# Attention values with the exp tiles as stationary operand, V plus a column of ones moving, one normalisation per token, DMA transposes, and three feed-forward PSUM banks

## Chip, cores, metric

One core of a Trainium2 chip. The metric is device microseconds of one execution. "PE" is the tensor engine, "PEld" its weight loads, "DVE" the vector engine, "ACT" the scalar engine, "POOL" GpSimd, "SP" the queue that issues nearly all DMAs. SBUF is the memory in which the tiles lie, PSUM the one that the matmuls write to, dealt out in banks. A matmul has a stationary operand (lhsT in the code), put in place by a weight load, and a moving one (rhs); "columns" are those of the moving one. A quad is four heads of one batch.

## The reference

Batch 4, 8 heads, 768 tokens, head size 64, 16 cluster centroids per head; then a gated feed-forward block on 3072 tokens of width 512.

```python
q_assign = argmax(q_n @ c_n.T);  k_assign = argmax(k_n @ c_n.T)      # per head
scores   = where(q_assign == k_assign, q @ k.T / 8, -1e9)
attn     = exp(scores - max) ;  attn /= attn.sum(-1) + 1e-9
x        = (attn @ v), heads side by side                            # [3072, 512]
out      = (silu(x @ w_gate) * (x @ w_val)) @ w_out                  # d_ff = 1536
```

## The kernel before

Work is cut into 192 units (batch, half of the queries, head, pair of key blocks), 48 to a batch and 24 to a chunk of 384 tokens. A unit is two score matmuls, one exp, and the value matmuls of the unit before it. The feed-forward block of chunk n runs between the units of chunk n+1, so PE always has both kinds of work in its queue. Before a batch's units there is preparation of q and k (transposes, cluster routing, masks).

The value product, with V stationary and the 384 exp columns moving. V stands beside 64 columns of ones, so the denominator comes out already copied to 64 partitions. A 385th column, filled with a tiny constant, sums V for rows in which every key is masked:

```python
def att_values(u, pt):
    ...
    for jj in range(2):
        j = 2 * kp + jj
        nc.tensor.matmul(
            out=acc[:, 0:SH + 1], lhsT=va[:, h % 4, 2 * (j % JH) + j // JH, :],
            rhs=pt[:, jj, 0:SH + 1], start=(j == 0), stop=(j == J - 1))
    if kp == JH - 1:                      # once per head
        ...
        nc.scalar.activation(out=den[n0:n0 + 64], in_=acc[d0:d0 + 64, 0:SH],
                             func=ACT.Identity, bias=eps[d0:d0 + 64])
        nc.vector.tensor_scalar_add(num[n0:n0 + 64], acc[n0:n0 + 64, 0:SH],
                                    acc[n0:n0 + 64, SH:SH + 1])
        if h % 2 == 1: norms.append((num, den, (2 * b + hf) % XR, h // 2))

def normalise(num, den, xc, m):           # once per head pair
    for r in range(JH):
        nc.vector.reciprocal(out=den[:, ts(r, 128)], in_=den[:, ts(r, 128)])
        yield                             # one per unit
    nc.gpsimd.tensor_tensor(out=xall[:, xc, m, :], in0=num, in1=den, op=ALU.mult)
```

Gate and value share a pair of PSUM banks, drawn from the same three pairs as the scores and the preparation:

```python
def ffn_gv(ch, fb):
    gv = psum.tile([128, 2, 512], FP32, name="gv", tag="big", bufs=3)
    # 4 matmuls into gv[:, 0], 4 into gv[:, 1]; then
    # ACT: th = tanh(gv0/2);  DVE: ug = (th+1)*gv0;  DVE: hT = ug*gv1
```

The softmax here doesn't subtract the row's maximum and nothing guards it: scores larger than these inputs give would overflow.

Of the kernel before, what the change touches and what calls it, by code (L numbers as in the profile page):

```python
# [17 lines left out]
def kernel(  # L18
# [32 lines left out]
    XR = 4  # L51
# [17 lines left out]
    def load_quad(qi):  # L69
        b, g = quads[qi]  # L70
        for i in range(4):
            h = 4 * g + i
            ts_ = []
            for src in (q, k):
                t = sb.tile([128, J, 64], FP32, name="qk", tag="qk", bufs=12)
                nc.sync.dma_start(
                    out=t, in_=src[b, h].rearrange("(p j) d -> p j d", p=128))
                ts_.append(t)
            qk_tiles[(b, h)] = ts_

    for s in range(2):
# [7 lines left out]
    NV = 3  # L89
    vaugs = [persist.tile([128, 4, J, 128], BF16, name=f"vaug{i}")  # L90
             for i in range(NV)]

    vst = {}

    def load_v(qi):
        b, g = quads[qi]
        va = vaugs[qi % NV]
        if qi < NV:
            vr = va.rearrange("p (a t) j c -> p a t j c", t=2)
            nc.gpsimd.memset(vr[:, :, 0, :, 64:128], 1.0)  # L100
            nc.gpsimd.memset(vr[:, :, 1, :, 0:64], 1.0)
        for i in range(4):
            t = sb.tile([128, J, 64], FP32, name="vs", tag="vs", bufs=4)
# [5 lines left out]
    def cast_v(qi, i):  # L109
        c0 = 64 * (i % 2)  # L110
        copy(nc.scalar if qi == 0 else nc.gpsimd,
             vaugs[qi % NV][:, i, :, c0:c0 + 64], vst.pop((qi, i)))
# [6 lines left out]
    pts = [persist.tile([128, 2, SH + 2], BF16, name=f"pt{i}")  # L119
           for i in range(NP)]  # L120
    for i in range(NP):
        nc.vector.memset(pts[i][:, :, SH:SH + 2], TINY)
    eps = persist.tile([128, 1], FP32, name="eps")
    nc.vector.memset(eps, S * TINY)
# [32 lines left out]
    def cast_w(i):  # L157
        eng = nc.vector if i % 3 == 0 else nc.gpsimd
# [13 lines left out]
    def prep_head(qi, i):  # L172
# [3 lines left out]
        tp = psum.tile([128, 2, 512], FP32, name="tp", tag="big", bufs=3)  # L176
# [19 lines left out]
    def prep_route(qi):  # L196
        b, g = quads[qi]
        sp = psum.tile([128, 2, 512], FP32, name="sp", tag="big", bufs=3)
# [31 lines left out]
    def prep_mask(qi, i):  # L230
        b, g = quads[qi]
        for par in range(2):
            nc.vector.tensor_copy(  # L233
                out=qkaug[(b, 4 * g + i)][D:KA, par],
                in_=ohTs[qi][32 * i:32 * i + NCL, par])
# [4 lines left out]
    def att_scores(u):  # L240
        b, hf, h, kp = u
        sc = psum.tile([128, 2, 512], FP32, name="sc", tag="big", bufs=3)
# [10 lines left out]
        nc.scalar.activation(out=pt[:, :, 0:SH], in_=sc[:, :, 0:SH],  # L253
# [5 lines left out]
    def att_values(u, pt):  # L259
# [3 lines left out]
        if kp == 0:  # L263
            accs[(b, hf, h)] = psum.tile([128, 512], FP32, name="acc",
                                         tag="acc", bufs=2)
        acc = accs[(b, hf, h)]
        for jj in range(2):
            j = 2 * kp + jj
            nc.tensor.matmul(  # L269
                out=acc[:, 0:SH + 1], lhsT=va[:, h % 4, 2 * (j % JH) + j // JH, :],  # L270
                rhs=pt[:, jj, 0:SH + 1], start=(j == 0), stop=(j == J - 1))
        if kp == JH - 1:
            del accs[(b, hf, h)]
            n0 = 64 * (h % 2)
            d0 = 64 - n0
            if h % 2 == 0:
                st["num"] = sb.tile([128, SH], FP32, name="num",
                                    tag="num", bufs=2)
                st["den"] = sb.tile([128, SH], FP32, name="den",
                                    tag="den", bufs=2)  # L280
            num, den = st["num"], st["den"]
            nc.scalar.activation(  # L282
                out=den[n0:n0 + 64], in_=acc[d0:d0 + 64, 0:SH],
                func=ACT.Identity, bias=eps[d0:d0 + 64])
            nc.vector.tensor_scalar_add(  # L285
                num[n0:n0 + 64], acc[n0:n0 + 64, 0:SH],
                acc[n0:n0 + 64, SH:SH + 1])
            if h % 2 == 1:
                norms.append((num, den, (2 * b + hf) % XR, h // 2))

    norms = []

    def normalise(num, den, xc, m):
        for r in range(JH):
# [186 lines left out]
```

## Time and profile before

| | before |
|---|---|
| time, median | 402.85 us at first; 401.5 to 403.1 on the later chips |
| PE, DVE, ACT, POOL busy | 368, 298, 276, 116 us |
| units 48 to 96 (one batch) | 92.6 us |

The page: busy time of each engine, then busy tenths in 40 slices of the span (9 is 90% or more; PEclk is the granted tensor clock), the main DMA queue, and the engines' shares of the chain of work that ended last.

```profile
span 400.8 us, 6063 instructions
...
PE 367.8 (92%) x2147; PEld 204.2 (51%) x2161; DVE 297.8 (74%) x498; ACT 275.9 (69%) x416; POOL 115.6 (29%) x144
...
PE   7868886799998999999999999999999999999996
...
DVE  4999879959688639869878648977958663866680
...
PEclk9989999999999999999999999999999999999999
DMA  8987888433200241152200111000100001000102
...
q1 hardware_dynamic: 25248, 34.61, 26.1%
...
PE 61%; DVE 20%; ACT 10%; DMA 3%; POOL 2%; issue 2%; SPq 0%; POOLq 0%; ACTq 0%
...
```

PE is at 9 in nearly every slice from the tenth on; only the first 90 us show slack, and there the DMA engines are busy.

The cost groups of the normalisation (count, then busy us and mean ns, then idle time before them):

```profile
...
L295 DVE RECIPROCAL den<-den 128x128 f32<-128x128 f32 x96 | 86.6, 930 | 0.5
...
L285 DVE TENSOR_SCALAR num<-acc 64x384 f32<-64x384 f32 x64 | 39.8, 622 | 34.7 <-ACT den L282 33.7
...
L282 ACT ACTIVATE den<-acc,eps 64x384 f32<-64x384 f32 x64 | 36.9, 576 | 5.5 <-PE acc L269 4.0
L298 POOL TENSOR_TENSOR xall<-num,den 128x384 bf16<-128x384 f32 x32 | 32.0, 999 | 148.5 <-DVE den L295 120.8 <-DVE ug L324 12.3 <-ACT th L321 9.8
...
```

DVE spends 86.6 us on reciprocals of a denominator that stands in 64 equal copies. Together with the num and den lines, normalisation costs DVE 126 us and ACT 37 us.

Busy time of each engine by stage. The stretches are units 0 to 48 with the preparation ahead of them, units 48 to 96, 96 to 144, 144 to the last unit, and the tail:

```profile
...
core 0: us, PE busy (x) PEld busy (x) DVE busy (x) ACT busy (x) POOL busy (x), PEclk, DMA share, GB/s
0.00:99.00 99.00, 80.08 (x475) 43.63 (x477) 82.30 (x137) 67.85 (x100) 57.57 (x74) 0.98 0.70 230
99.00:191.60 92.60, 89.20 (x533) 50.41 (x536) 70.13 (x119) 67.84 (x103) 25.27 (x32) 1.00 0.22 69
191.60:284.00 92.40, 89.28 (x534) 50.47 (x536) 70.06 (x119) 67.92 (x103) 23.81 (x29) 1.00 0.08 29
284.00:367.10 83.10, 79.52 (x452) 44.14 (x454) 58.79 (x98) 61.72 (x94) 7.67 (x8) 1.00 0.05 20
367.10:400.80 33.70, 29.73 (x161) 15.59 (x160) 16.48 (x28) 10.53 (x20) 1.32 (x2) 0.99 0.13 47
...
```

In the second and third stretch PE is busy 89 of 92.5 us. But the records of successive matmuls overlap (0.33 us long and 0.163 us apart, see below), so I count from start to start instead. The timeline of PE, merged:

```profile
...
109.37 0.49 PE L269 MATMUL acc<-pt_132,vaug_95 128*128 128x385 bf16 x2
...
110.67 0.81 PE L316 MATMUL gv<-xall,wv_sb 128*128 128x384 bf16 x4
...
```

Two 385-column matmuls take 0.49 us, of which the last one's own record is 0.33: 0.163 us apart. Four of 384 columns take 0.81: also 0.163 apart. A 512-column one is 0.216 from the next, an fp32 transpose 0.108, and sixteen fp32 routing matmuls take 1.43 us. For one batch: 96 score matmuls 15.6 us, 96 value matmuls 15.65, 192 gate and value 31.2, 72 output 15.55, 48 transposes and 32 routing matmuls 8.1. That is 86.1 us of streaming, which leaves 6.5 of the 92.6 us as waits. The wait view of PE in that stretch names less than half of it (total us, times, longest):

```profile
...
PE gv L311 <- ACT pt_132 L253: 1.2, 3, 0.6
PE sc L246 <- DVE hT L327: 0.7, 2, 0.6
PE gv L311 <- DVE hT L327: 0.5, 1, 0.5
PE o_ps L336 <- DVE num L285: 0.4, 2, 0.2
```

As far as the view names them (2.8 of the 6.5 us), PE waits for PSUM banks, most of them of gate and value.

### The profile page before, as it was taken

The page shows a single profiled execution, that of the slowest core. Times are in us where ns is not written, and L with a number is a line of the kernel's source. Part 1 is how long each engine was busy: PE and PEld are TensorE (multiplying, and loading weights), DVE is VectorE, ACT ScalarE, POOL GpSimd, SP SyncE. Part 2 cuts the span into 40 slices and gives each one's busy share as a digit, 9 for nine tenths or more (in the row PEclk, how much of TensorE's full clock was granted, in tenths as well). Part 3 has the DMA queues.
Part 4 walks back from the last instruction along what each step waited for, and adds up shares of the span by engine and source line. Part 5 has one row for each costly group of instructions (what it writes and reads, how often), then busy time and mean ns, then how long its engine had stood idle before and what let it go on. Part 6 is the DMA issues. An engine that isn't in the chain of part 4 may idle for free.

```text
span 400.8 us, 6063 instructions
## 1 busy us (share of the span) xinstructions
PE 367.8 (92%) x2147; PEld 204.2 (51%) x2161; DVE 297.8 (74%) x498; ACT 275.9 (69%) x416; POOL 115.6 (29%) x144
## 2 busy tenths in 40 slices
PE   7868886799998999999999999999999999999996
PEld 4334433464555655565455654565455545554552
DVE  4999879959688639869878648977958663866680
ACT  6569955576677776786687686786777777766331
POOL 7863872553100351263101151244001001010000
PEclk9989999999999999999999999999999999999999
DMA  8987888433200241152200111000100001000102
GB/s 268 344 284 255 262 263 285 134 98 101 77 2 1 77 134 49 38 155 79 76 28 0 42 65 53 2 0 2 52 28 1 2 27 52 2 0 29 52 2 79
DMA packets 25567, 35.07 MB, mean 88 GB/s; under 512 B 2496, under 2 KB 20928, under 8 KB 25536
## 3 DMA queue, kind: packets, MB, share of 16 engines
q1 hardware_dynamic: 25248, 34.61, 26.1%
q8 instruction: 17, 0.28, 0.3%
q14 instruction: 14, 0.11, 0.1%
q10 hardware_dynamic: 288, 0.07, 0.1%
HBM read 28.38 MB, written 6.29 MB: 87 GB/s over the span
## 4 chain that ended last, share of the span: by engine, by line
PE 61%; DVE 20%; ACT 10%; DMA 3%; POOL 2%; issue 2%; SPq 0%; POOLq 0%; ACTq 0%
PE o_ps L336 13%; PE gv L311 12%; PE gv L316 12%; PE sc L246 10%; PE acc L269 10%; DVE den L295 5%; ACT pt_132 L253 4%; DVE qka L233 4%; PE tp L179 3%; DVE num L285 2%; PE sp L201 2%; DVE ug L324 2%; DVE hT L327 2%; DVE ohT L225 2%; ACT den L282 2%
## 5 line engine op out<-in xcount | busy, mean ns | idle before, releaser
L246 PE MATMUL sc<-qka 80*128 80x384 bf16 x384 | 93.6, 328 | 8.0 <-DVE sT L207 2.7
L311 PE MATMUL gv<-xall,wg_sb 128*128 128x384 bf16 x384 | 78.3, 325 | 11.5 <-ACT pt_132 L253 3.9
L295 DVE RECIPROCAL den<-den 128x128 f32<-128x128 f32 x96 | 86.6, 930 | 0.5
L324 DVE SCALAR_TENSOR_TENSOR ug<-th,gv 128x384 f32<-128x384 f32 x96 | 51.8, 540 | 41.6 <-ACT th L321 40.8
L321 ACT ACTIVATE th<-gv 128x384 f32<-128x384 f32 x96 | 47.2, 492 | 49.8 <-PE gv L316 48.7
L316 PE MATMUL gv<-xall,wv_sb 128*128 128x384 bf16 x384 | 78.1, 326 | 0.0
L298 POOL TENSOR_TENSOR xall<-num,den 128x384 bf16<-128x384 f32 x32 | 32.0, 999 | 148.5 <-DVE den L295 120.8
L336 PE MATMUL o_ps<-wo_sb,hT 128*128 128x512 bf16 x274 | 64.7, 379 | 1.6 <-DVE num L285 1.0
L285 DVE TENSOR_SCALAR num<-acc 64x384 f32<-64x384 f32 x64 | 39.8, 622 | 34.7 <-ACT den L282 33.7
L167 POOL CAST qka<-qkT 64x768 bf16<-64x768 f32 x60 | 51.9, 867 | 43.8 <-ACT qkT L183 42.1
L311 PEld LDWEIGHTS <-wg_sb 128*128 128x128 bf16 x384 | 36.9, 96 | 42.9 <-issue 18.7
L246 PEld LDWEIGHTS <-qka 80*128 80x128 bf16 x384 | 37.4, 99 | 35.8 <-issue 12.8
L327 DVE TENSOR_TENSOR hT<-ug,gv 128x384 bf16<-128x384 f32 x96 | 52.0, 543 | 2.4
L316 PEld LDWEIGHTS <-wv_sb 128*128 128x128 bf16 x384 | 37.5, 98 | 26.5 <-issue 1.7
L253 ACT ACTIVATE pt_135<-sc 128x768 bf16<-128x768 f32 x48 | 38.9, 810 | 8.2 <-PE sc L246 7.4
L336 PEld LDWEIGHTS <-hT 128*128 128x128 bf16 x288 | 28.0, 97 | 31.4
L253 ACT ACTIVATE pt_133<-sc 128x768 bf16<-128x768 f32 x48 | 38.9, 809 | 6.1 <-PE sc L246 5.9
L253 ACT ACTIVATE pt_132<-sc 128x768 bf16<-128x768 f32 x48 | 39.0, 812 | 5.1 <-PE sc L246 4.6
L253 ACT ACTIVATE pt_134<-sc 128x768 bf16<-128x768 f32 x48 | 39.0, 812 | 4.7 <-PE sc L246 3.1
L282 ACT ACTIVATE den<-acc,eps 64x384 f32<-64x384 f32 x64 | 36.9, 576 | 5.5 <-PE acc L269 4.0
L340 ACT ACTIVATE o_sb<-o_ps 128x512 f32<-128x512 f32 x24 | 14.3, 597 | 30.7 <-PE o_ps L336 30.7
L183 ACT ACTIVATE qkT<-tp 128x768 f32<-128x768 f32 x32 | 25.9, 811 | 8.9 <-PE tp L179 8.1
(75 smaller groups left out, 324.2 us busy)
## 6 DMA issues: line engine op xcount, KB each, us to landing
qk<-in_q_dram SPq DMA_DIRECT2D x32, 192.0 KB, 3.6
qk<-in_k_dram SPq DMA_DIRECT2D x32, 192.0 KB, 3.6
vs<-in_v_dram SPq DMA_DIRECT2D x32, 192.0 KB, 3.9
out_dram<-o_sb SPq DMA_DIRECT2D x24, 256.0 KB, 2.0
wt<-in_moe_w_gate_dram SPq DMA_DIRECT2D x6, 512.0 KB, 4.9
wt<-in_moe_w_val_dram SPq DMA_DIRECT2D x6, 512.0 KB, 4.5
wt<-in_moe_w_out_dram SPq DMA_DIRECT2D x6, 512.0 KB, 4.1
cn<-in_centroids_dram ACTq DMA_DIRECT2D x2, 32.0 KB, 2.9
```

The lines of the kernel that those rows point to most:

```text
L167: eng.tensor_copy(out=out, in_=in_)
L246: nc.tensor.matmul(out=sc[:, jj, 0:SH], lhsT=qka[:, j // JH, 1, ts(j % JH, 128)], rhs=qka[:, hf, 0, :], start=True, stop=True)
L253: nc.scalar.activation(out=pt[:, :, 0:SH], in_=sc[:, :, 0:SH], func=ACT.Exp, scale=SCALE)
L282: nc.scalar.activation(out=den[n0:n0 + 64], in_=acc[d0:d0 + 64, 0:SH], func=ACT.Identity, bias=eps[d0:d0 + 64])
L285: nc.vector.tensor_scalar_add(num[n0:n0 + 64], acc[n0:n0 + 64, 0:SH], acc[n0:n0 + 64, SH:SH + 1])
L295: nc.vector.reciprocal(out=den[:, ts(r, 128)], in_=den[:, ts(r, 128)])
L311: nc.tensor.matmul(out=gv[:, 0, 0:SH], lhsT=wg_sb[:, c, ts(fb, 128)], rhs=xall[:, cb, c, :], start=(c == 0), stop=(c == DMC - 1))
L316: nc.tensor.matmul(out=gv[:, 1, 0:SH], lhsT=wv_sb[:, c, ts(fb, 128)], rhs=xall[:, cb, c, :], start=(c == 0), stop=(c == DMC - 1))
L321: nc.scalar.activation(out=th, in_=gv[:, 0, 0:SH], func=ACT.Tanh, scale=0.5)
L324: nc.vector.scalar_tensor_tensor(out=ug, in0=th, scalar=1.0, in1=gv[:, 0, 0:SH], op0=ALU.add, op1=ALU.mult)
L327: nc.vector.tensor_tensor(out=hTs[ch][:, fb, :], in0=ug, in1=gv[:, 1, 0:SH], op=ALU.mult)
L336: nc.tensor.matmul(out=o_ps, lhsT=hT[:, fc, ts(ob, 128)], rhs=wo_sb[:, fc, :], start=(fc == 0), stop=(fc == DFC - 1))
```

## The change

The intent: make the exp tile the stationary operand and let 65 columns (V and one column of ones) move. A unit's two 385-column matmuls become six of 65 columns. The result has tokens on partitions, so the denominator is one number per token and head: six reciprocals per partition in place of 384. The result must then be turned; 32 DMA transposes from SBUF to SBUF do that. Freed PSUM is dealt out anew: two bank pairs for scores and preparation, one accumulator bank for a head pair, three single banks for gate, value and output. The masked-row correction, formerly the 385th column, becomes a sum of V per quad of heads (sum_v). Some casts and mask copies move between DVE, ACT and POOL.

```diff
+    def sum_v(qi):
+        nc.vector.tensor_reduce(out=vs1, in_=vaugs[qi % NV].rearrange("p i j c -> p i c j"), ...)
+        nc.tensor.matmul(out=vp, lhsT=ones_f, rhs=vs1..., start=True, stop=True)
+        nc.vector.tensor_scalar_mul(vsb[qi % NV]..., vp, TINY)
 ...
         for jj in range(2):
             j = 2 * kp + jj
-            nc.tensor.matmul(
-                out=acc[:, 0:SH + 1], lhsT=va[:, h % 4, 2 * (j % JH) + j // JH, :],
-                rhs=pt[:, jj, 0:SH + 1], start=(j == 0), stop=(j == J - 1))
+            for a in range(JH):
+                nc.tensor.matmul(
+                    out=acc[:, h % 2, a, :], lhsT=pt[:, jj, ts(a, 128)],
+                    rhs=va[:, h % 4, 2 * (j % JH) + j // JH, :],
+                    start=(h % 2 == 0 and j == 0 and a == 0),
+                    stop=(j == J - 1), skip_group_check=True)
 ...
-            nc.scalar.activation(out=den..., func=ACT.Identity, ...)
-            nc.vector.tensor_scalar_add(num...)
-        for r in range(JH): nc.vector.reciprocal(out=den..., in_=den...)
+    def normalise(acc, qi, xc, m):                       # once per head pair
+        nc.vector.tensor_tensor(out=num, in0=acc, in1=vsb[...]..., op=ALU.add)
+        nc.vector.reciprocal(out=rec, in_=num[:, :, :, D:D + 1])
+        nc.gpsimd.tensor_tensor(out=xn..., in0=num[:, :, :, 0:D], in1=rec..., op=ALU.mult)
+        nc.sync.dma_start_transpose(out=xall[:, xc, m, :]..., in_=xn...)
 ...
-        gv = psum.tile([128, 2, 512], FP32, name="gv", tag="big", bufs=3)
+        if ch == NCH - 1 and fb % 5 in (1, 3):           # last chunk: borrow a score pair
+            gv = psum.tile([128, 2, 512], FP32, name="gv", tag="sc", bufs=2)
+        else:
+            gp = psum.tile([128, 512], FP32, name="gp", tag="f", bufs=3)
+            vp = psum.tile([128, 512], FP32, name="vp", tag="f", bufs=3)
 ... (tags, buffer counts, XR 4 -> 2, engines of casts and mask copies: cut)
```

More of the change, by code (lines that the diff above doesn't have):

```diff
@@ L50 @@
     NCH = 2 * B
-    XR = 4
+    XR = 2
     persist = ctx.enter_context(tc.tile_pool(name="persist", bufs=1))
@@ L74, in load_quad @@
             for src in (q, k):
-                t = sb.tile([128, J, 64], FP32, name="qk", tag="qk", bufs=12)
+                t = sb.tile([128, J, 64], FP32, name="qk", tag="qk", bufs=16)
                 nc.sync.dma_start(
@@ L89 @@
     NV = 3
-    vaugs = [persist.tile([128, 4, J, 128], BF16, name=f"vaug{i}")
+    vaugs = [persist.tile([128, 4, J, D + 1], BF16, name=f"vaug{i}")
              for i in range(NV)]
+    vsb = [persist.tile([128, 4, D + 1], FP32, name=f"vsb{i}")
+           for i in range(NV)]
+    ones_f = persist.tile([128, 128], FP32, name="ones_f")
+    nc.gpsimd.memset(ones_f, 1.0)
     vst = {}
@@ L98, in load_v @@
         if qi < NV:
-            vr = va.rearrange("p (a t) j c -> p a t j c", t=2)
-            nc.gpsimd.memset(vr[:, :, 0, :, 64:128], 1.0)
-            nc.gpsimd.memset(vr[:, :, 1, :, 0:64], 1.0)
+            nc.gpsimd.memset(va[:, :, :, D:D + 1], 1.0)
         for i in range(4):
-            t = sb.tile([128, J, 64], FP32, name="vs", tag="vs", bufs=4)
+            t = sb.tile([128, J, 64], FP32, name="vs", tag="vs", bufs=8)
             nc.sync.dma_start(
@@ L109, in cast_v @@
     def cast_v(qi, i):
-        c0 = 64 * (i % 2)
         copy(nc.scalar if qi == 0 else nc.gpsimd,
-             vaugs[qi % NV][:, i, :, c0:c0 + 64], vst.pop((qi, i)))
+             vaugs[qi % NV][:, i, :, 0:D], vst.pop((qi, i)))
+    def sum_v(qi):
+        vs1 = sb.tile([128, 4, D + 1], FP32, name="vs1", tag="vs1", bufs=1)
+        nc.vector.tensor_reduce(
+            out=vs1, in_=vaugs[qi % NV].rearrange("p i j c -> p i c j"),
+            axis=AX.X, op=ALU.add)
+        vp = psum.tile([128, 4 * (D + 1)], FP32, name="vsp", tag="f", bufs=3)
+        nc.tensor.matmul(out=vp, lhsT=ones_f,
+                         rhs=vs1.rearrange("p i c -> p (i c)"),
+                         start=True, stop=True)
+        nc.vector.tensor_scalar_mul(
+            vsb[qi % NV].rearrange("p i c -> p (i c)"), vp, TINY)
     load_quad(1)
@@ L118 @@
     NP = 4
-    pts = [persist.tile([128, 2, SH + 2], BF16, name=f"pt{i}")
+    pts = [persist.tile([128, 2, SH], BF16, name=f"pt{i}")
            for i in range(NP)]
-    for i in range(NP):
-        nc.vector.memset(pts[i][:, :, SH:SH + 2], TINY)
-    eps = persist.tile([128, 1], FP32, name="eps")
-    nc.vector.memset(eps, S * TINY)
     nc.vector.memset(c_nT, 0.0)
@@ L157, in cast_w @@
     def cast_w(i):
-        eng = nc.vector if i % 3 == 0 else nc.gpsimd
+        eng = nc.vector if i in (0, 1) else nc.gpsimd
         eng.tensor_copy(out=wjobs[i][1], in_=wst.pop(i))
@@ L175, in prep_head @@
         qn, kn = qk_tiles.pop((b, h))
-        tp = psum.tile([128, 2, 512], FP32, name="tp", tag="big", bufs=3)
+        tp = psum.tile([128, 2, 512], FP32, name="tp", tag="sc", bufs=2)
         for t, src in enumerate((qn, kn)):
@@ L197, in prep_route @@
         b, g = quads[qi]
-        sp = psum.tile([128, 2, 512], FP32, name="sp", tag="big", bufs=3)
+        sp = psum.tile([128, 2, 512], FP32, name="sp", tag="sc", bufs=2)
         for t in range(2):
@@ L232, in prep_mask @@
         for par in range(2):
-            nc.vector.tensor_copy(
-                out=qkaug[(b, 4 * g + i)][D:KA, par],
-                in_=ohTs[qi][32 * i:32 * i + NCL, par])
+            copy(nc.scalar if qi == 0 and i == 0 and par == 0
+                 else nc.gpsimd if qi == 1 else nc.vector,
+                 qkaug[(b, 4 * g + i)][D:KA, par],
+                 ohTs[qi][32 * i:32 * i + NCL, par])
     st = {"np": 0}
@@ L241, in att_scores @@
         b, hf, h, kp = u
-        sc = psum.tile([128, 2, 512], FP32, name="sc", tag="big", bufs=3)
+        sc = psum.tile([128, 2, 512], FP32, name="sc", tag="sc", bufs=2)
         qka = qkaug[(b, h)]
@@ L252, in att_scores @@
         st["np"] += 1
-        nc.scalar.activation(out=pt[:, :, 0:SH], in_=sc[:, :, 0:SH],
+        nc.scalar.activation(out=pt, in_=sc[:, :, 0:SH],
                              func=ACT.Exp, scale=SCALE)
@@ L262, in att_values @@
         va = vaugs[qi % NV]
-        if kp == 0:
-            accs[(b, hf, h)] = psum.tile([128, 512], FP32, name="acc",
-                                         tag="acc", bufs=2)
-        acc = accs[(b, hf, h)]
+        if kp == 0 and h % 2 == 0:
+            accs[(b, hf)] = psum.tile([128, 2, JH, D + 1], FP32, name="acc",
+                                      tag="acc", bufs=1)
+        acc = accs[(b, hf)]
         for jj in range(2):
             j = 2 * kp + jj
-            nc.tensor.matmul(
-                out=acc[:, 0:SH + 1], lhsT=va[:, h % 4, 2 * (j % JH) + j // JH, :],
-                rhs=pt[:, jj, 0:SH + 1], start=(j == 0), stop=(j == J - 1))
@@ L272, in att_values @@
-        if kp == JH - 1:
-            del accs[(b, hf, h)]
-            n0 = 64 * (h % 2)
-            d0 = 64 - n0
-            if h % 2 == 0:
-                st["num"] = sb.tile([128, SH], FP32, name="num",
-                                    tag="num", bufs=2)
-                st["den"] = sb.tile([128, SH], FP32, name="den",
-                                    tag="den", bufs=2)
-            num, den = st["num"], st["den"]
-            nc.scalar.activation(
-                out=den[n0:n0 + 64], in_=acc[d0:d0 + 64, 0:SH],
-                func=ACT.Identity, bias=eps[d0:d0 + 64])
-            nc.vector.tensor_scalar_add(
-                num[n0:n0 + 64], acc[n0:n0 + 64, 0:SH],
-                acc[n0:n0 + 64, SH:SH + 1])
-            if h % 2 == 1:
-                norms.append((num, den, (2 * b + hf) % XR, h // 2))
@@ L291 @@
-    norms = []
-    def normalise(num, den, xc, m):
-        for r in range(JH):
-            nc.vector.reciprocal(out=den[:, ts(r, 128)],
-                                 in_=den[:, ts(r, 128)])
-            yield
-        nc.gpsimd.tensor_tensor(out=xall[:, xc, m, :], in0=num, in1=den,
-                                op=ALU.mult)
+            for a in range(JH):
[4 more added lines that the diff above has]
+                    stop=(j == J - 1), skip_group_check=True)
@@ new lines, in att_values @@
+        if kp == JH - 1 and h % 2 == 1:
+            del accs[(b, hf)]
+            normalise(acc, qi, (2 * b + hf) % XR, h // 2)
+    def normalise(acc, qi, xc, m):
+        num = sb.tile([128, 2, JH, D + 1], FP32, name="num", tag="num", bufs=2)
+        i0 = 2 * (m % 2)
+        nc.vector.tensor_tensor(
+            out=num, in0=acc,
+            in1=vsb[qi % NV][:, i0:i0 + 2, :].unsqueeze(2).to_broadcast(
+                [128, 2, JH, D + 1]), op=ALU.add)
+        rec = sb.tile([128, 2, JH, 1], FP32, name="rec", tag="rec", bufs=2)
+        nc.vector.reciprocal(out=rec, in_=num[:, :, :, D:D + 1])
+        xn = sb.tile([128, JH, 2, D], BF16, name="xn", tag="xn", bufs=2)
+        nc.gpsimd.tensor_tensor(
+            out=xn.rearrange("p a h d -> p h a d"), in0=num[:, :, :, 0:D],
+            in1=rec.to_broadcast([128, 2, JH, D]), op=ALU.mult)
+        nc.sync.dma_start_transpose(
+            out=xall[:, xc, m, :].rearrange("p (a t) -> p a t", a=JH),
+            in_=xn.rearrange("p a h d -> p (a h d)"))
@@ L308, in ffn_gv @@
                               bufs=2)
-        gv = psum.tile([128, 2, 512], FP32, name="gv", tag="big", bufs=3)
-        for c in range(DMC):
-            nc.tensor.matmul(out=gv[:, 0, 0:SH],
-                             lhsT=wg_sb[:, c, ts(fb, 128)],
-                             rhs=xall[:, cb, c, :],
-                             start=(c == 0), stop=(c == DMC - 1))
-        for c in range(DMC):
-            nc.tensor.matmul(out=gv[:, 1, 0:SH],
-                             lhsT=wv_sb[:, c, ts(fb, 128)],
-                             rhs=xall[:, cb, c, :],
-                             start=(c == 0), stop=(c == DMC - 1))
+        if ch == NCH - 1 and fb % 5 in (1, 3):
+            gv = psum.tile([128, 2, 512], FP32, name="gv", tag="sc", bufs=2)
+            gp, vp = gv[:, 0, 0:SH], gv[:, 1, 0:SH]
+        else:
+            gp = psum.tile([128, 512], FP32, name="gp", tag="f", bufs=3)
+            vp = psum.tile([128, 512], FP32, name="vp", tag="f", bufs=3)
+            gp, vp = gp[:, 0:SH], vp[:, 0:SH]
+        for dst, w in ((gp, wg_sb), (vp, wv_sb)):
+            for c in range(DMC):
+                nc.tensor.matmul(out=dst, lhsT=w[:, c, ts(fb, 128)],
+                                 rhs=xall[:, cb, c, :],
+                                 start=(c == 0), stop=(c == DMC - 1))
         th = sb.tile([128, SH], FP32, name="th", tag="th", bufs=3)
-        nc.scalar.activation(out=th, in_=gv[:, 0, 0:SH], func=ACT.Tanh,
-                             scale=0.5)
+        nc.scalar.activation(out=th, in_=gp, func=ACT.Tanh, scale=0.5)
         ug = sb.tile([128, SH], FP32, name="ug", tag="ug", bufs=3)
         nc.vector.scalar_tensor_tensor(
-            out=ug, in0=th, scalar=1.0, in1=gv[:, 0, 0:SH],
-            op0=ALU.add, op1=ALU.mult)
-        nc.vector.tensor_tensor(out=hTs[ch][:, fb, :], in0=ug,
-                                in1=gv[:, 1, 0:SH], op=ALU.mult)
+            out=ug, in0=th, scalar=1.0, in1=gp, op0=ALU.add, op1=ALU.mult)
+        nc.vector.tensor_tensor(out=hTs[ch][:, fb, :], in0=ug, in1=vp,
+                                op=ALU.mult)
     outr = out.rearrange("(b p j) d -> b j p d", b=B, j=J)
@@ L333, in ffn_out @@
         hT = hTs[ch]
-        o_ps = psum.tile([128, 512], FP32, name="o_ps", tag="acc", bufs=2)
+        o_ps = psum.tile([128, 512], FP32, name="o_ps", tag="f", bufs=3)
         for fc in range(DFC):
@@ L344, in centroids_T @@
     def centroids_T():
-        ctp = psum.tile([128, 128], FP32, name="ctp", tag="acc", bufs=2)
+        ctp = psum.tile([128, 128], FP32, name="ctp", tag="f", bufs=3)
         nc.tensor.transpose(out=ctp, in_=cn.rearrange("p s d -> p (s d)"),
@@ L356, in warm @@
     def warm(n):
-        wp = psum.tile([128, 256], FP32, name="wp", tag="acc", bufs=2)
+        wp = psum.tile([128, 256], FP32, name="wp", tag="f", bufs=3)
         for i in range(n):
@@ L398 @@
         put(n, *f)
+    put(4, sum_v, 0)
     for i in range(4):
         put(4 + i, cast_v, 1, i)
+    put(8, sum_v, 1)
     for i in range(len(wjobs)):
@@ L411 @@
             put(u0 + 3 * NU // 2 + 5 + i, cast_v, NQ * b + 1, i)
+        put(u0 + 12, sum_v, NQ * b)
+        put(u0 + 3 * NU // 2 + 9, sum_v, NQ * b + 1)
         put(u0 + 22, load_quad, NQ * b + 1)
@@ L417 @@
             put(u0 + (36 + 2 * n if n < 5 else 42 + n), *f)
-    run = []
-    def step_norm():
-        for g in list(run):
-            if next(g, 0) == 0:
-                run.remove(g)
-        while norms:
-            run.append(normalise(*norms.pop(0)))
     pend = None
@@ L442 @@
             f[0](*f[1:])
-        step_norm()
         if ui == 2:
@@ L446 @@
     att_values(*pend)
-    while norms or run:
-        step_norm()
     for f in fw[fpos:]:
```

## The prediction

> **What bounds the kernel now.** The tensor engine. In the slice table PE is busy 0.97 from 93 us to the tail; over one batch (93.2 to 185.9 us, 92.7 us) the window table gives PE 89.3, DVE 70.2, ACT 67.9, POOL 25.3 us. Start to start in the trace, a 384-column bf16 matmul takes 0.163 us, a 512-column one 0.216, an fp32 transpose 0.108. Summed for one batch: scores 15.6, values 15.7, gate and value 31.2, output 15.6, preparation 8.1: 86.2 of 92.7 us. The waits view names only about 3 us of PE waits in that batch. The first 93 us are different: PE is busy 74 us, DMA 0.92 then 0.80 of its time until 63 us, DVE and POOL 0.6 to 0.85.
>
> **What changes.**
> - PE: per unit two 385-column value matmuls (0.326 us) become six of 65 columns, each with its own weight load; in all 384 become 1152. At the measured rate 65 columns stream in 27 ns plus 2.5. The disputed term is the weight load. The trace shows a load beginning when the preceding matmul begins and hidden behind 162 ns; exposed, the matmul starts 4 to 44 ns after its load, and narrow loads start 7 ns apart. [...]
> - DVE: reciprocals (96 x 0.93 = 86.6 us) and num (64 x 0.62 = 39.8) go. Estimated from like shapes: one add of 390 elements 0.55 us and a 6-element reciprocal 0.17 us, 32 times (23 us); the V sums 8 x 2.3 us (18). Net -85 us; further casts and mask copies go to POOL.
> - ACT: den copies (64 x 0.58 = 36.9 us) go.
> - POOL: the product stays about 1 us x32; four weight casts (1.04 us each) and eight mask copies come, memsets (4.4 us) go.
> - DMA: 32 transposes SBUF to SBUF, 98 KB each. Plain loads of 192 KB land in 3.6 us; I estimate 2 to 4 us. In steady state a chunk needs none of them at once.
> - PSUM: one accumulator bank instead of two, two score pairs, three single FFN banks. New waits are possible, but DVE is then under 0.5 busy, so evacuation is prompt.
>
> **On the critical path.** DVE and ACT relief is mostly off it, because PE is the limit. From 93 us to the tail the PE saving counts: 148 units x 0.086 = 13 us, plus about 5 us of waits. In the first 93 us DVE relief lets chunk 0 run faster, but DMA and the two-buffer weight pipeline hold it: 7 us. The tail is unchanged. 402.9 - 25 = 378 us.
>
> **Prediction.** 378 us, 8 in 10 between 360 and 394. Faster by over 2%: 0.83; within 2%: 0.12; slower: 0.05.
>
> **What would show it.** [...]one batch about 87 us; DVE near 210, ACT near 239 us busy; transposes landing in 2 to 4 us; PE still over 0.9 busy; few PE waits on num or hT.
>
> **What would make it wrong.** [...]PE waiting at every head pair on the single accumulator; transposes that are slow or block the sync queue, holding back loads or chunk starts; POOL saturated in the first 60 us.

The cuts take out what the forecast allowed for a pair of weight load and matmul at 65 columns, and the steps and two tests that rest on it: six pairs were taken as 0.24 us per unit, so 0.086 of the 0.326 saved. That was the estimate, and no run shows it (measured, below: 0.177 us). The forecast's sum came to 13 (148 x 0.086) + 5 + 7 = 25 us, and 402.9 - 25 = 378 us. Its "27 ns plus 2.5" is the line through the trace's 162.5 ns at 384 columns and 215.8 at 512. Its "like shapes" stand in the same trace: 0.54 us for a product of 384 elements on DVE, 0.16 for a reciprocal of one. For the 2.3 us of a V sum the trace has only a maximum over 768 elements, 0.95 us; at that rate 1560 take 1.9, so 2.3 is an estimate that the trace does not give.

## The result, and the profile after

| | before | after |
|---|---|---|
| time, median (same chip) | 401.74 us (400.12 to 404.27) | 372.06 us (371.88 to 373.92) |
| ratio, 95% interval | | 0.9266 (0.9204 to 0.9329) |
| DVE, ACT busy | 298, 276 us | 221, 232 us |

A ratio here and below is the mean time of one kernel's runs over that of the other's of the same rounds, so it is not quite the ratio of the medians quoted. Executions over 1.5% slower than the fastest of the same kernel are left out of the means. Where kernels of different chips are compared, I compare their ratios to the kernel before and turn a difference of ratios into us with 402 us.

The page after:

```profile
span 370.2 us, 7635 instructions
...
PE 345.4 (93%) x2928; PEld 207.7 (56%) x2945; DVE 220.6 (60%) x400; ACT 232.3 (63%) x353; POOL 117.3 (32%) x154
...
PE   8748886999999999999999999999999999999995
...
DVE  3898419675976516875976525874846613660670
...
PEclk9967996799999999999999999999999999999999
DMA  7977798879220143234020012000120012001102
...
q1 hardware_dynamic: 38560, 37.76, 32.7%
...
PE 73%; DVE 12%; DMA 6%; POOL 3%; ACT 3%; issue 2%; SPq 0%; ACTq 0%; DVEq 0%; POOLq 0%
...
xall<-xn SPq DMA_TRANSPOSE x32, 2.3
```

DVE has come down from 74% to 60% and ACT from 69% to 63%, yet PE's share has hardly moved and its share of the chain has grown from 61% to 73%. The clock row holds 6 or 7 in four of the first eight slices: the trace has two stretches of 10.2 us at half clock (21.5 to 31.8 and 59.1 to 69.3 us), where before had one of 3.4 us. The last line is the new transpose group: 32 of them, landing in 2.3 us at the median (3 of the 32 took over 4 us).

The normalisation's cost groups after (one of three num forms and one of eight reductions):

```profile
...
L299 POOL TENSOR_TENSOR xn<-num,rec 128x384 bf16<-128x384 f32 x32 | 27.1, 846 | 137.3 <-DVE rec L297 99.0 <-issue 36.2 <-POOL qka L176 2.1
...
L292 DVE TENSOR_TENSOR num<-acc,vsb_97 128x390 f32<-128x390 f32 x12 | 6.7, 560 | 18.9 <-PE acc L280 18.8
...
L297 DVE RECIPROCAL rec<-num 128x6 f32<-128x6 f32 x32 | 6.0, 186 | 0.4
...
L117 DVE TENSOR_REDUCE vs_390<-vaug_93 128x260 f32<-128x1560 bf16 x1 | 2.9, 2852 | 0.0
...
```

The reciprocals cost 6 us, the product on POOL 27 us (32 before). The reduction for the V sum takes 2.9 us each time, eight times over.

By stage, same columns as before:

```profile
...
0.00:96.80 96.80, 80.78 (x671) 47.59 (x673) 64.77 (x106) 60.14 (x85) 63.20 (x84) 0.89 0.81 259
96.80:180.80 84.00, 82.01 (x731) 50.64 (x733) 53.41 (x99) 56.19 (x87) 24.08 (x32) 1.00 0.27 79
180.80:264.90 84.10, 82.10 (x734) 50.73 (x736) 53.54 (x100) 56.34 (x87) 22.55 (x29) 1.00 0.10 29
264.90:336.50 71.60, 70.98 (x641) 43.15 (x642) 35.36 (x73) 49.53 (x79) 6.67 (x8) 1.00 0.12 34
336.50:370.20 33.70, 29.56 (x170) 15.54 (x168) 13.52 (x26) 10.14 (x19) 0.82 (x1) 0.99 0.14 50
...
```

| stretch | before | after | difference |
|---|---|---|---|
| to the first score matmul | 18.4 | 18.5 | +0.1 |
| units 0 to 48 | 80.6 | 78.3 | -2.3 |
| units 48 to 96 | 92.6 | 84.0 | -8.6 |
| units 96 to 144 | 92.4 | 84.1 | -8.3 |
| unit 144 to the last score matmul | 83.1 | 71.6 | -11.5 |
| tail | 33.7 | 33.7 | 0.0 |

All but 2 of the 30.6 us come from the stages in which PE is the limit. The timeline of PE there:

```profile
...
130.60 0.48 PE L256 MATMUL sc<-qka 80*128 80x384 bf16 x2
130.93 0.35 PE L280 MATMUL acc<-vaug_93,pt_135 128*128 128x65 bf16 x6
...
```

Six value matmuls take 0.35 us, of which the last one's record is 0.19: about 30 ns apart. Over all 963 adjacent pairs the median is 29 ns. So a unit's six take 0.177 us (at 29.5 ns; a unit's six in a row start 30.4 ns apart at the median) in place of 0.326, and one batch's values 8.5 us in place of 15.65. With 0.9 us for two V sums (each stands in the trace as two 260-column fp32 matmuls; the second is 0.22 us from the next matmul, and I count that twice) a batch streams 79.9 us, and 84.0 - 79.9 leaves 4.1 us of waits where there were 6.5. The wait view of PE for units 48 to 96 has one line left:

```profile
...
PE vp L323 <- DVE ug L329: 1.4, 3, 0.7
```

Nothing waits for the single accumulator bank.

So by arithmetic a batch's 8.6 us are 6.2 of streaming and 2.4 of waits. That invites a simple theory, which I call **A**: the gain is streaming time, and the relief of DVE and ACT is a small extra. Rivals are **R**, the relief is most of it, and **P**, the new PSUM layout is most of the rest.

### The profile page after: what moved, and what is told of

Read it like the earlier page. It is cut to its first block, busy times and chain, and to the rows that moved or that the text cites. A ratio compares the mean times of both kernels' runs of the same rounds, so it can differ in the third digit from the quotient of the medians.

```text
span 370.2 us, 7635 instructions
## 1 busy us (share of the span) xinstructions
PE 345.4 (93%) x2928; PEld 207.7 (56%) x2945; DVE 220.6 (60%) x400; ACT 232.3 (63%) x353; POOL 117.3 (32%) x154
## 3 DMA queue, kind: packets, MB, share of 16 engines
q1 hardware_dynamic: 38560, 37.76, 32.7%
## 4 chain that ended last, share of the span: by engine, by line
PE 73%; DVE 12%; DMA 6%; POOL 3%; ACT 3%; issue 2%; SPq 0%; ACTq 0%; DVEq 0%; POOLq 0%
PE vp L323 15%; PE o_ps L340 15%; PE sc L256 14%; PE gp L323 14%; PE acc L280 8%; DMA wt<-in_moe_w_val_dram 3%; PE tp L188 3%; DVE qka L176 3%; PE sp L210 2%; POOL qka L176 2%; DVE ohT L234 2%; PE gv L323 2%; ACT pt_135 L263 2%; DVE ug L329 1%; DMA xall<-xn 1%
## 5 line engine op out<-in xcount | busy, mean ns | idle before, releaser
L329 DVE SCALAR_TENSOR_TENSOR ug<-th,gp 128x384 f32<-128x384 f32 x91 | 50.2, 552 | 71.9 <-ACT th L327 71.7
L323 PE MATMUL vp<-xall,wv_sb 128*128 128x384 bf16 x364 | 76.0, 331 | 3.6 <-DVE ug L329 3.6
L323 PE MATMUL gp<-xall,wg_sb 128*128 128x384 bf16 x364 | 76.1, 328 | 2.5 <-DMA xall<-xn 2.5
L299 POOL TENSOR_TENSOR xn<-num,rec 128x384 bf16<-128x384 f32 x32 | 27.1, 846 | 137.3 <-DVE rec L297 99.0
L331 DVE TENSOR_TENSOR hT<-ug,vp 128x384 bf16<-128x384 f32 x91 | 50.2, 553 | 8.4 <-PE vp L323 1.0
L327 ACT ACTIVATE th<-gp 128x384 f32<-128x384 f32 x91 | 44.6, 491 | 7.8 <-PE gp L323 7.8
L263 ACT ACTIVATE pt_136<-sc 128x768 bf16<-128x768 f32 x48 | 38.7, 807 | 11.5 <-PE sc L256 10.9
L256 PEld LDWEIGHTS <-qka 80*128 80x128 bf16 x384 | 28.7, 101 | 20.8 <-issue 11.2
L344 ACT ACTIVATE o_sb<-o_ps 128x512 f32<-128x512 f32 x24 | 14.3, 597 | 36.1 <-PE o_ps L340 33.7
L188 PE MATMUL tp<-ident_f,qk 128*128 128x128 f32 x192 | 27.5, 279 | 0.9 <-ACT qkT L192 0.3
L176 DVE COPY qka<-ohT 16x768 bf16<-16x768 bf16 x55 | 25.8, 494 | 0.9
L188 PEld LDWEIGHTS tp<-ident_f,qk 128*128 128x128 f32 x192 | 20.5, 141 | 3.2 <-issue 0.9
```

The lines of the kernel that those rows point to most:

```text
L176: eng.tensor_copy(out=out, in_=in_)
L188: nc.tensor.transpose(out=tp[:, t, ts(a, 128)], in_=src[:, 2 * a:2 * a + 2, :], identity=ident_f)
L256: nc.tensor.matmul(out=sc[:, jj, 0:SH], lhsT=qka[:, j // JH, 1, ts(j % JH, 128)], rhs=qka[:, hf, 0, :], start=True, stop=True)
L263: nc.scalar.activation(out=pt, in_=sc[:, :, 0:SH], func=ACT.Exp, scale=SCALE)
L299: nc.gpsimd.tensor_tensor(out=xn.rearrange("p a h d -> p h a d"), in0=num[:, :, :, 0:D], in1=rec.to_broadcast([128, 2, JH, D]), op=ALU.mult)
L323: nc.tensor.matmul(out=dst, lhsT=w[:, c, ts(fb, 128)], rhs=xall[:, cb, c, :], start=(c == 0), stop=(c == DMC - 1))
```

## The experiments

| kernel | ratio to before (95%) | against before | streaming, waits of PE in units 48 to 96 |
|---|---|---|---|
| before | 1 | 0 | 86.1 + 6.5 = 92.6 |
| after | 0.9266 (0.9204 to 0.9329) | -29.5 us | 79.9 + 4.1 = 84.0 |
| b_relief | 0.9793 (0.9753 to 0.9832) | -8.3 | 86.1 + 5.1 = 91.2 |
| b_narrow | 0.9748 (0.9707 to 0.9788) | -10.1 | 79.1 + 9.9 = 89.0 |
| b_both | 0.9236 (0.9180 to 0.9292) | -30.7 | 79.1 + 6.0 = 85.1 |
| a_double | 1.0093 (1.0048 to 1.0137) | +3.7 | 88.4 + 4.2 = 92.6 |
| a_bank | 0.9446 (0.9401 to 0.9491) | -22.3 | 79.9 + 6.1 = 86.0 |
| a_dve2 | 0.9375 (0.9347 to 0.9404) | -25.1 | 79.9 + 6.0 = 85.9 |
| a_dve | 0.9745 (0.9682 to 0.9808) | -10.3 | 91.8 in all; not a fair test, see below |
| a_nosum | 0.9107 (0.9069 to 0.9146) | -35.9 | 79.0 + 3.2 = 82.2 |
| a_pesum | 0.9132 (0.9094 to 0.9170) | -34.9 | 80.3 + 3.3 = 83.6 |
| a_route | 0.9286 (0.9240 to 0.9331) | -28.7 | no fast profile |
| a_pesum_route | 0.9245 (0.9219 to 0.9270) | -30.4 | 83.5 in all |

Streaming is counted as above; waits are the rest of the measured stretch. The kernels named b_ start from the kernel before, those named a_ from the changed one. Outside the first units the order of instructions on an engine is not that of the program text (20 of a_dve's 192 dummies started before the first score matmul, see below), so each edit may also shift that order a little. The number of feed-forward blocks done by every twelfth unit agrees to within two blocks. No run isolates the relief of ACT from that of DVE, or the other edits of the change (casts and mask copies on other engines, more load buffers).

### b_relief: take the DVE and ACT work away, keep the wide matmuls

```diff
-            nc.scalar.activation(out=den..., in_=acc..., func=ACT.Identity, ...)
+            num = den = st["num"]
-        for r in range(JH):
-            nc.vector.reciprocal(out=den[:, ts(r, 128)], in_=den[:, ts(r, 128)])
-            yield
+        yield
```

> The kernel before, wide value matmuls kept, with the 96 reciprocals (86.6 us of DVE) and the 64 denominator copies (36.9 us of ACT) left out; the result is wrong on purpose. Theory A (the gain is tensor-engine streaming time, the relief of DVE and ACT only shortens waits): 3 to 10 us faster than before, about 395 us, PE matmul time unchanged. Rival R (the gain is mostly the relief of DVE and ACT): 20 to 30 us faster, near 375 us.

Measured: 393.2 us, 8.3 us faster, result wrong. Inside theory A's range, far from R's. DVE fell to 222 us, as low as in the changed kernel, and a batch gained only 1.4 us:

```profile
...
94.10:185.30 91.20, 88.91 (x533) 50.47 (x536) 52.00 (x95) 58.59 (x87) 23.80 (x32) 1.00 0.22 70
...
```

Of the rest, 5.0 us were gained before unit 48 (75.6 us in place of 80.6).

### b_narrow: shorten PE's value work, keep the DVE and ACT work

```diff
-                out=acc[:, 0:SH + 1], ..., rhs=pt[:, jj, 0:SH + 1], ...
+                out=acc[:, 0:n], ..., rhs=pt[:, jj, 0:n], ...   # n = 385 if j == 0 else 170
```

> The kernel before with DVE and ACT work untouched, but five of the six value matmuls of a head cut from 385 to 170 columns, so that a head's value matmuls take 0.53 us of PE as 18 narrow pairs at 29.5 ns do in the changed kernel, in place of 0.98; wrong result on purpose. Theory A: at least 18 of the 30 us are gained, 375 to 384 us. Rival R: under 8 us gained, because DVE and ACT hold the stages.

Measured: 391.5 us, 10.1 us faster, wrong result. **Theory A fell here**: it asked for at least 18 us. (R, which allowed under 8, does not hold either.) The window line and the waits of PE for units 48 to 96:

```profile
...
97.60:186.60 89.00, 82.93 (x535) 48.57 (x537) 70.15 (x119) 67.08 (x103) 24.99 (x32) 1.00 0.22 72
...
```

```profile
...
PE gv L312 <- ACT pt L253: 2.2, 4, 0.8
PE gv L312 <- ACT qkT L183: 1.3, 2, 0.6
PE gv L312 <- DVE hT L328: 1.0, 2, 0.7
...
```

PE streams 7.0 us less per batch, but the batch shrinks by only 3.6: waits rise from 6.5 to 9.9 us. The lines that grew are gate matmuls that wait for their bank pair, held by exp, by the preparation copy or by the last product (the view names 5.6 of the 9.9 us). DVE and ACT have the same work as before in less time.

The new theory, **A2**: the streaming saving is real, but without relief about half of it turns into waits for the shared banks; relief alone has little to shorten; only both together pay.

### b_both: the two parts together

> The kernel before with both parts at once: no reciprocals and no denominator copies, and the narrow value matmuls; old PSUM layout, no transposes, no V sums; wrong result on purpose. Alone the two gave 8.3 and 10.0 us. If they simply add: about 383 us. Theory A2 (narrow matmuls alone lose half of their 28 us to waits for gate and value banks that DVE and ACT hold, and the relief gives that half back): 372 to 378 us, and in units 48 to 96 PE waits of about 6.5 us per batch as against 9.9 with the narrow matmuls alone.

Measured: 372.7 us, 30.7 us faster. Adding 8.3 and 10.1 would have given 18.4. The window line for units 48 to 96:

```profile
...
91.80:176.90 85.10, 81.94 (x539) 48.43 (x537) 51.66 (x95) 58.14 (x87) 23.77 (x32) 1.00 0.24 75
...
```

The relief is worth 1.4 us per batch beside wide matmuls (92.6 to 91.2), and 3.9 beside narrow ones (89.0 to 85.1). Waits are back at 6.0 us. A2's forecast holds.

That b_both, with the old PSUM layout, no transposes and no V sums, reaches the changed kernel's total is partly luck. From unit 48 to the last score matmul the stage times add up to 268.1 us in before, 264.1 in b_relief, 257.0 in b_narrow, 245.6 in b_both and 239.7 in the changed kernel. There too the two parts together gain more (22.5 us) than their sum (4.0 + 11.1), but the changed kernel gains 5.9 more. Ahead of unit 48 it is the other way round: b_both gains 7.6 us, the changed kernel 2.3.

### a_double: issue each narrow matmul twice

```diff
-            for a in range(JH):
+            for a, r in [(a, r) for a in range(JH) for r in range(2)]:
 ... (start and stop set for the doubled order: cut)
```

> The changed kernel with every 65-column value matmul issued twice into the same accumulator (numerator and denominator double together, so the result stays right). 1152 more load-and-matmul pairs. Theory A: each costs its 29.5 ns on the critical path, so 30 to 36 us slower than the changed kernel, about 404 us, back at before. If PE had slack, under 15 us. If the weight load were near its limit, the pairs would spread to over 35 ns.

Measured: 405.3 us, correct; 0.0827 in ratio, or 33 us, above the changed kernel: 29 ns for each of the 1152 pairs. 1152 times 29.5 ns is 34 us. Units 48 to 96 took 92.6 us, 8.6 more, where 288 extra pairs predict 8.5. Streaming time of PE now counts in full.

### a_bank: the changed kernel with the old PSUM layout

```diff
-        sc = psum.tile([128, 2, 512], FP32, name="sc", tag="sc", bufs=2)
+        sc = psum.tile([128, 2, 512], FP32, name="sc", tag="big", bufs=3)   # also tp, sp, gv
-            accs[(b, hf)] = psum.tile(..., tag="acc", bufs=1)
+            accs[(b, hf)] = psum.tile(..., tag="acc", bufs=2)               # also o_ps
```

> The changed kernel with the PSUM layout of before: three shared bank pairs for preparation, scores, and gate and value, and two single banks for accumulator and output. Rival P (the three FFN banks and separate score pairs give a good part of the gain by taking PE waits away): 8 us or more slower than the changed kernel. Theory A: within 4 us of it either way; and since three pairs let two more score pairs run while a routing result waits, the first 12 units take about 13 us as before and not 17.

Measured: 378.8 us, 7.2 us slower than the changed kernel, correct. Between what the two theories asked for, so the sharp forms of both fail. The window line for units 48 to 96:

```profile
...
94.60:180.60 86.00, 82.82 (x734) 50.86 (x736) 52.99 (x99) 57.94 (x87) 23.93 (x32) 1.00 0.27 77
...
```

The new layout is worth 2.0 us in that batch (86.0 against 84.0), 1.9 in the next and 3.9 from unit 144 on. At the start it costs: units 0 to 12 take 14.4 us with the old layout and 17.0 with the new. So the layout, taken away by itself, is about a quarter of the gain. Without it the changed kernel needs 247.5 us from unit 48 to the last score matmul, close to b_both's 245.6, as A2 would have it.

### a_dve and a_dve2: put DVE work back

The first try put six dummy reciprocals per head pair on DVE, on a scratch tile that nothing else touches.

```diff
+        for r in range(2 * JH):
+            nc.vector.reciprocal(out=csq, in_=csq)
```

> The changed kernel with six 64-element dummy reciprocals per head pair on DVE (about 0.5 us each, 90 to 100 us in all), which brings DVE back to about 310 us busy, with nothing waiting for their result but what stands behind them on DVE. Theory A2: they cost 4 to 10 us, through gate and value banks held longer. If DVE relief were the main gain: 15 us or more. If it were worth nothing: under 2 us.

Measured: 391.9 us, ratio 0.9745, 19 us slower than the changed kernel, which would speak for R. But the experiment was not what I had meant. DVE's slices, from the page:

```profile
...
DVE  6999976999997999999998899887574631662570
...
```

Work that depends on nothing was placed as early as DVE had room: 20 of the 192 had started before the first score matmul (the expectation of a_dve2 below says 25), which came at 23.0 us and not at 18.5, and none was left after 250 us. They took 0.55 us each, 104.8 in all. In units 48 to 96 DVE was busy 87.3 of 91.8 us, in the kernel before 70.1 of 92.6. **Inconclusive.** The repair ties three reciprocals per head pair (0.94 us each, 90.0 in all) to that pair's numerators, one per unit, as the old kernel's were:

```diff
+        dums.append(num)          # then, one per unit:
+                nc.vector.reciprocal(out=wz[:, 0:128]..., in_=num[:, :, r, 0:D])
```

> Repair of a_dve, whose dummies waited for nothing and were placed up to 25 deep ahead of the first attention unit. The changed kernel with three reciprocals of 384 numerators per head pair (about 0.93 us each, 89 us in all), tied to that pair's numerators, one per unit, as the old kernel's were; their result is not read. Theory A2: 4 to 10 us slower than the changed kernel, on this chip's scale 376 to 384 us if before is about 402. If 15 us or more, DVE relief is a main gain by itself; under 2 us, it is worth nothing.

Measured: 377.4 us, correct, 4.4 us slower than the changed kernel. Window line for units 48 to 96:

```profile
...
98.00:183.90 85.90, 83.03 (x740) 50.78 (x736) 71.48 (x123) 56.27 (x87) 24.15 (x32) 1.00 0.28 77
...
```

DVE is back at 71.5 us per batch, as before the change, and the batch costs 1.9 us more (85.9 against 84.0). With the new PSUM layout the same DVE load does less harm than the 3.9 us that it and ACT's copies do with the old. Inside A2's range.

### a_nosum and a_pesum: the V sums

a_nosum forms the V sum only once. The correction has a weight of 2 to the power -100, so on this data the result stays right.

```diff
-    put(8, sum_v, 1)
-        put(u0 + 12, sum_v, NQ * b)
-        put(u0 + 3 * NU // 2 + 9, sum_v, NQ * b + 1)
-        in1=vsb[qi % NV]...
+        in1=vsb[0]...
```

> The changed kernel with only the first of the eight V sums (2.9 us of DVE each and one fp32 matmul); all quads use the first one's. It enters with weight 2 to the power -100, so the result stays right on this data. Theory S2 (three sums in the first 40 us are part of why the start gained little): 1 to 4 us faster, most of it before unit 48. Rival: the sums lie in idle DVE time: within 1 us.

Measured: 367.2 us, 6.4 us faster than the changed kernel, somewhat more than I expected. Units 0 to 48 took 74.7 us (after: 78.3), units 48 to 96 took 82.2 (84.0). Seven reductions of 2.9 us on an engine that is 60% busy, with their fp32 matmuls, were therefore not free: about 0.9 us each. In units 48 to 96 half of the 1.8 us is the streaming of those matmuls (79.9 - 79.0), half is waits (4.1 - 3.2). The waits show in the trace: in the changed kernel PE's value matmuls stand 0.68 us waiting for a product on DVE right after the sum at 159.8 us, and again after that at 243.8 us; a_nosum has no wait of that length there. The other two sums of those batches (102.0 and 186.1 us) are followed by none.

a_pesum keeps all eight sums and forms them on PE:

```diff
-        nc.vector.tensor_reduce(out=vs1, in_=vaugs[qi % NV]..., axis=AX.X, op=ALU.add)
-        nc.tensor.matmul(out=vp, lhsT=ones_f, rhs=vs1..., start=True, stop=True)
-        nc.vector.tensor_scalar_mul(vsb[qi % NV]..., vp, TINY)
+        for j in range(J):
+            nc.tensor.matmul(out=vp, lhsT=tiny_b, rhs=vaugs[qi % NV][:, :, j, :],
+                             start=(j == 0), stop=(j == J - 1))
+        nc.vector.tensor_copy(out=vsb[qi % NV]..., in_=vp)
```

> The changed kernel with the V sums on the tensor engine: six accumulating bf16 matmuls of 260 columns with a constant 2 to the power -100 as stationary operand, about 0.67 us per quad, in place of a 2.9 us DVE reduction and two fp32 passes (0.44 us). Leaving seven sums out gave about 6 us; so 3 to 6 us faster than the changed kernel, ratio to before 0.912 to 0.920, and correct. If the gain of a_nosum had come from the matmul and not from DVE: within 1 us.

Measured: 367.5 us, correct, ratio 0.9132; 5.4 us faster than the changed kernel, and the interval does not touch the changed kernel's. **This version beats both kernels.** It gives PE more work (0.67 us per quad, an estimate from the start-to-start times at 384 and 512 columns, in place of 0.44) and DVE less. Most of the gain lies at the start: units 0 to 48 took 74.7 us in place of 78.3, units 48 to 96 took 83.6 in place of 84.0.

### a_route and a_pesum_route: the start

The changed kernel's first twelve units take 17.0 us, the old ones 13.1. The timelines of PE and DVE there:

```profile
...
23.74 0.80 PE L256 MATMUL sc<-qka 80*128 80x384 bf16 x2 [4.74 <-DVE sT L216]
...
```

```profile
...
16.32 6.36 DVE L176 COPY qka<-ohT 16x768 bf16<-16x768 bf16 x7
22.70 0.98 DVE L216 STREAM_TRANSPOSE sT<-sp 128x768 f32<-128x768 f32 x1
```

The score matmuls wait 4.74 us for a bank pair that routing holds, until DVE reads it at 22.7 us, behind seven mask copies that take 6.4 us. Each of the seven took 0.88 to 0.98 us, because it began while POOL was casting q and k; with POOL idle the same copy takes 0.35 (last section). I moved that routing behind the third score unit.

```diff
-    for f in prep(0)[5:] + prep(1)[4:5]:
+    for f in prep(0)[5:]:
         f[0](*f[1:])
+    put(2, *prep(1)[4])
 ... (the mask copies that follow it go three units later too: cut)
```

> The changed kernel with the routing of the second quad issued after the third score unit and not before the first, so that its score bank pair is not held while DVE copies the masks of the first quad. Theory S (the first 12 units lose about 4 us to that held pair: one wait of 4.7 us, after which the tensor clock runs at half for 10 us): units 0 to 12 shrink from 17 us to 13 us or less, the half-clock stretch at 21 to 32 us is gone, and the whole is 2 to 5 us faster than the changed kernel, 367 to 370 us. Rival: DMA and the weight pipeline hold the start, and it is within 1 us.

Measured: three runs of 373.1 to 375.6 us, ratio 0.9286, no gain. The profiled run, very slow (1218 us), says nothing of the start; it is left out. Whether units 0 to 12 got shorter could not be seen, so I tried it again on a_pesum.

> a_pesum with the later routing of the second quad. a_route by itself was within noise of the changed kernel and its only profile fell in a very slow state. If the start is held by something else (weights and POOL), the time is within 1 us of a_pesum and units 0 to 12 get shorter while 12 to 36 get longer by as much. If the held pair still costs, 2 to 4 us faster than a_pesum.

Measured: 372.1 us, on the same chip as a_pesum's 367.5: 4.6 us slower. Both guesses were wrong. Units 0 to 12 did not shrink (19.7 us, a_pesum 18.5), units 0 to 48 grew from 74.7 to 80.2. The waits of PE, first of a_pesum in 18 to 38 us, then of a_pesum_route in 0 to 60 us:

```profile
...
PE vsp L118 <- POOL vaug L172: 7.1, 2, 7.0
...
```

```profile
...
PE vsp L118 <- POOL vaug L172: 4.9, 1, 4.9
PE vsp L118 <- POOL qka L172: 2.6, 1, 2.6
...
```

In both, PE starts nothing else while it stands at the second V sum (from 19.3 to 26.2 us in a_pesum). POOL casts the last of the V that it reads only after eight casts of q and k, which take 7.5 us in either kernel. With the later routing PE stands 2.6 us at the first sum as well; the view names POOL's first cast of q and k (ended at 17.76 us), but that sum reads V, whose last cast ended on ACT at 17.72. The held pair was the wait that showed, not the limit: take it away and PE stands at the next item whose input is late. Time at half clock goes with it: 27 us in a_pesum_route's trace, 7 in a_pesum's, 20 in the changed kernel's. But a_nosum has low mean clocks too (0.955 to 0.979) and is as fast as a_pesum (0.988 to 0.990), and b_both, with 17 us at half clock, has the shortest first stage of all (73.0 us), so the clock is not shown to be the cause.

### a_probe: what one load-and-matmul pair costs

Behind the last block, 48 pairs each of 16, 32, 65, 128 and 256 columns, a different 128x128 bf16 stationary tile each time.

> The changed kernel with 48 load-and-matmul pairs each of 16, 32, 65, 128 and 256 columns added behind the last block, on the last chunk's data, results not read. Theory A (the load hides behind the preceding matmul): [...]29.5 at 65, 56 at 128, 109 at 256. [...]

One look, in a single run of unknown state (383.8 us); granted clock 1.0 in the stretch. Median start to start, worked out from the start times in the trace:

| columns | 16 | 32 | 65 | 128 | 256 |
|---|---|---|---|---|---|
| ns | 25 | 25 | 29 | 56 | 109 |

The load, 96 to 98 ns long by its record, is longer than the step from start to start at 16 to 128 columns. At 65, 128 and 256 columns the line through the 162.5 ns at 384 columns and the 215.8 at 512 (before) gives 30, 56 and 109 ns, an estimate that leaves no time for the load: there it is hidden. At 16 and 32 columns the line gives 9 and 16, and both took 25; what sets those 25 ns is not shown.

## Why the prediction was right, and where its steps were not

- **Time and range: right.** 378 us were predicted, 372.1 measured; the range was 360 to 394.
- **A unit's six pairs at 0.24 us, 40 ns a pair: mis-sized.** A pair measured 29 ns in the kernel and in the probe. The 40 were the estimate, which no run showed; in the trace of the kernel before, loads hide (97 ns long, begun 160 ns ahead of their matmul). The unit saves 0.149 us and not 0.086. Over the 148 units from 44 on that is 22 us and not 13, less 1.8 us for the matmuls of four V sums. (The "4 to 44 ns" are three value matmuls of the kernel before, which started 4, 31 and 44 ns after their own loads, at 50.4, 45.0 and 48.2 us. Nothing rests on it.)
- **"DVE and ACT relief is mostly off it [the critical path]": wrong, the weakest step.** The sum came out well although its logic did not: that was luck. The savings set too low (22 us and not 13, and 9 us of waits and not 5) made up for the V sums' matmuls and for the start, which was set too high (2 us and not 7). b_narrow gained 10 us and b_relief 8; together they gained 31. I had treated the streaming saving as counting in full by itself. Without the relief only half of it counts (a batch shrank by 3.6 us for 7.0 us less streaming); with it and the new layout, all (a_double).
- **"about 5 us of waits": mis-sized.** Waits fell by 2.4 us in units 48 to 96, by 8.3 - 6.2 = 2.1 in the next batch and, without V sums there, by 11.5 - 47 x 0.149 = 4.5 in the last stretch: 9 us. Taking away the PSUM layout, for which I had foreseen only possible new waits, costs 2.0 + 1.9 + 3.9 us there (a_bank), and giving DVE its work back costs 1.9 + 2.0 + 0.6 (a_dve2). In the two batches each alone undoes nearly the whole gain in waits, so both are needed and their shares cannot be added.
- **"In the first 93 us ... 7 us": mis-sized.** Units 0 to 48 gained 2.3 us, although their streaming fell by 7 (48 x 0.149). The waits that its trace names there are for the routing bank pair (4.7 us) and for the transposed x of the first chunk (2.2 us). b_both, without transposes and V sums and with the old layout, gained 7.6 there.
- **V sums "8 x 2.3 us", counted only as DVE load: wrong in kind.** They took 2.9 us each, and leaving seven out gained 6.4 us. Half of what they cost in units 48 to 96 was their own matmuls on PE, which the prediction left out.
- **Batch "about 87 us", DVE "near 210", ACT "near 239", DVE "under 0.5 busy":** 84.0, 221 and 232 us; in units 48 to 96 DVE was 0.64 busy (53.4 of 84.0 us).
- **Transposes "2 to 4 us", "the tail is unchanged", no wait on the accumulator bank: right.** They landed in 2.3 us at the median, the tail took 33.7 us both times, and no such wait is in the profile.

Open: what limits the first 48 units of the changed kernel. The experiments show that it is not the held routing pair alone, and that the V sums on DVE are 3.6 us of it.

## What to carry to other kernels

When one engine is the limit and its work shrinks, ask who hands its buffers back: a saving on the busy engine and relief of the engines that empty its banks can be worth far more together than apart (31 us against 8 and 10; in the stages where PE is the limit, 22.5 against 4 and 11). An operation of several microseconds on an engine with idle time need not be free when short operations that return buffers queue behind it (seven reductions of 2.9 us on a DVE that was 60% busy: 6.4 us); try it on another engine, even the busiest, if it is cheap there (on PE, a_pesum: 5.4 us faster). A dummy load used as an experiment must depend on what the real work depended on, or it may be done early, as it was here, and measure something else.

## What else the traces show

- Weight loads. In the kernel before, a load for gate or value begins 2 ns after the preceding matmul does (median), and its own matmul 160 ns after that. In the changed kernel the 2224 bf16 loads of the full 128 rows lasted 98 ns at the median, and 2023 of them began while the record of a matmul of the full height ran. A load-and-matmul pair took 29 ns at 65 columns, 56 at 128 and 109 at 256 (a_probe).
- One run (a_route's profile) took 1218 us with matmuls of 384 columns mostly 630 ns apart in place of 163 (their records 898 and 904 ns long for gate and value, 328 and 331 in the changed kernel), while exp still took 810 ns. Its trace holds no clock event at all, so the granted clock of 1.0 that is listed for it says nothing. The cause stays open.
- Transposes. From the DMA queue's line, the 32 transposes (37.76 - 34.61 = 3.15 MB) added 0.327 x 370.2 - 0.261 x 400.8 = 16.5 us of all 16 engines, an estimate of 191 GB/s, against 331 GB/s for the rest of the queue (34.61 MB in 104.6 us). The transposes move in packets of 256 bytes, the rest in 1 to 2 KB. The plain load of the centroids also moves in packets of 256 bytes, and a packet took 18 ns at the median in both. No run of this case has transposes in larger packets. One transpose also held the issuing queue for 1.19 us, a plain transfer for 0.34 to 0.39 (medians).
- Copies on DVE beside POOL. In the changed kernel the same 16x768 bf16 copy took 351 ns (median of 26) with POOL idle. The 16 copies that began well inside a POOL instruction (over 0.15 us before its end) took 500 to 1183 ns, and each ended 208 to 218 ns after that instruction; 11 that began before POOL's took 343 to 355. So these 16 waited POOL's instruction out.
